# A fused attention and expert kernel: first loads issued by three engines, zero matmuls at the start, the first two tiles closed earlier, and GpSimd's sums in pieces

## The chip, the cores and the metric

The kernel runs on one core of a Trainium2 chip. The metric is the device time of one execution in microseconds. Engines are named as the profile names them: PE is TensorE (with PEld for its weight loads), DVE is VectorE, ACT is ScalarE, POOL is GpSimd and SP is SyncE.

## What is computed

A sliding-window attention is followed by a layer of eight experts, of which each token goes to one. All is in float32.

```python
# q, k, v: (8, 8, 576, 64); window 64
scores = matmul(q, k.T) / sqrt(64);  mask = (rel >= 0) & (rel < 64)
attn = softmax(where(mask, scores, -1e9));  x = (attn @ v) as 4608 tokens x 512
logits = x @ w_gate;  expert = argmax(logits);  gate = softmax(logits)[expert]
for e in range(8):                       # w1: (8, 512, 1024), w2: (8, 1024, 512)
    y[tokens of e] = relu(x[tokens of e] @ w1[e]) @ w2[e]
out = gate * y
```

## The kernel before

**Attention.** The batch is cut into four groups of two sequences (bg = 0 to 3), each group into four units (one pair of heads), each unit into three rounds. That gives N = 48 rounds, and `step(s)` is a software pipeline over them: it scores round s + 1, weighs v for round s - 1, turns (transposes) the q and k of round s + 3, and does whatever stands in `todo` for s. The last 64 positions of each sequence, the "rests", are loaded for a whole group at once and are used by each unit's third round.

```python
def step(s):
    if 0 <= s + 1 < N:
        prs[s + 1] = softened(*masked(s + 1, scored(s + 1)))   # PE, DVE (L585), ACT (L595)
    if 0 <= s - 1 < N:
        px = weighted(s - 1, pTs.pop(s - 1))                   # PE (L618)
    ripe = 0 <= s - 3 < N and logit(s - 3)                     # PE (L655)
    if 0 <= s < N:
        pTs[s] = flipped(prs.pop(s))                           # PE (L603), DVE and ACT (L605)
    if 0 <= s - 1 < N:
        divided(s - 1, px)                                     # DVE (L628 to L632)
    ...                                                        # at each unit's first step: loads for u+2 and u+3
    if s + 3 < N:
        turned(s + 3)                                          # PE (L539, L531), ACT (L544, L534)
    if 0 <= s - 2 < N:
        x_turned(s - 2)                                        # PE (L643), ACT (L646)
    for op in todo.pop(s, ()):
        op()
    ...
load_qk(0); (wg and zrow); load_rests(0); load_v(0); load_qk(1); load_v(1); load_qk(2)   # all on SyncE
for s in range(-3, N):
    step(s)
```

`load_v` also has GpSimd copy each v to a second alignment (L511 to L517).

**Routing.** When a group's logits are known, `choose(bg)` (DVE) finds each token's expert and its rank among that expert's tokens; `place` (DVE, L746) makes a one-hot operand of the rank; `weigh` multiplies x by the gate; `store` writes x to DRAM. A tile is 256 tokens of one expert, in two halves of 128. The table that says which token stands in which slot is a series of small matmuls of those operands. Tiles 0 and 1 belong to expert 0 and are closed before the last group: the count of expert 0 is raised to 512 after the third group. Their table is made in step 45, and the tokens are fetched with an indirect DMA:

```python
def first_tiles():                       # todo of step N - 3
    V.scalar_tensor_tensor(out=key[:], ...)                    # L859
    V.tensor_tensor(out=hi_e[:], ..., op=ALU.is_equal)         # L862
    for j in range(NJE):                                       # 27 x 2 matmuls, L869
        for i in range(2):
            nc.tensor.matmul(slots, lhsT=lo[:, i, j], rhs=hi_e[:, j], ...)
    V.tensor_scalar(out=perm_e[:], in0=slots, ...)             # L872
    gather_first(perm_e[:, 0:C])                               # GpSimd: fill with zeros, indirect DMA
```

**Experts.** A tile goes through `turn` (transpose x), `sums_x`, `hidden` (x @ w1, relu) and `output` (@ w2). Both products are done with seven half-size products in place of eight, which needs sums of the quarters of x (DVE, L311), of w1 and w2 (GpSimd, L139) and of the hidden layer (DVE, L139):

```python
def left_sums(eng, s, a11, a12, a21, a22):
    for n, (a, b, op) in enumerate((
        (a21, a22, ALU.add), (s[:, 0], a11, ALU.subtract), (a11, a21, ALU.subtract),
        (a12, s[:, 1], ALU.subtract))):
        yield partial(eng.tensor_tensor, out=s[:, n], in0=a, in1=b, op=op)   # L139
def sums_w1(e): form(left_sums(G, s1s[e % NW], *w1q(e)))
def sums_w2(e): form(right_sums(G, s2s[e % NW], *w2q(e)))
```

After the loop of steps, tile 0's products are interleaved with the last group's routing and with the table of all further tiles (`slot_table`, matmuls L807). Then tile 1 follows, and a loop over the experts.

Of the kernel before, what the change touches and what calls it, by code (L numbers as in the profile page):

```python
# [4 lines left out]

# [31 lines left out]
def kernel(  # L37
# [44 lines left out]

    ident = consts.tile([P, P], F32, name="ident")
    make_identity(nc, ident[:])
    GE = 32
# [54 lines left out]

    def w1q(e):
        w = w1s[e % NW]
        return [w[:, a * HG : (a + 1) * HG, f * HD : (f + 1) * HD] for f in range(2) for a in range(2)]
# [5 lines left out]
    def sums_w1(e):  # L149
        form(left_sums(G, s1s[e % NW], *w1q(e)))  # L150

    def sums_w2(e):
        form(right_sums(G, s2s[e % NW], *w2q(e)))
# [59 lines left out]
    hi_e = rt.tile([P, NJE, NE * C], BF16, name="hi_e")  # L213
# [23 lines left out]
    ST = 3  # L237
# [39 lines left out]
    def gather_first(tokens):  # L277

        for c in range(C):
            G.memset(xg[c], 0.0)  # L280

            G.indirect_dma_start(
                out=xg[c], out_offset=None, in_=x_dram[0 : NT - BG * S, :],
                in_offset=bass.IndirectOffsetOnAxis(ap=tokens[:, c : c + 1], axis=0),
                bounds_check=NT - BG * S - 1, oob_is_err=False,
            )
# [12 lines left out]
    def turn():  # L299

        for c in range(C):
            for g in range(NG):
                nc.tensor.transpose(out=tps[c][:, g, :], in_=xg[c][:, g * P : (g + 1) * P], identity=ident[:])  # L303
            nc.scalar.copy(out=xq[:, :, c], in_=tps[c].rearrange("p (a g) s -> p a g s", a=2))
        yield

    def sums_x():

        b12, b22, b21 = tps[1][:, 0:HG], tps[1][:, HG:], tps[0][:, HG:]
        for n, (a, b) in enumerate(((b12, xq[:, 0, 0]), (b22, xs[:, 0]), (b22, xq[:, 0, 1]), (xs[:, 1], b21))):  # L310
            V.tensor_tensor(out=xs[:, n], in0=a, in1=b, op=ALU.subtract)  # L311
# [128 lines left out]
    with tc.manual_schedule(), ExitStack() as held, ExitStack() as brief:  # L440
# [6 lines left out]


        NM = 2 + ST
        mask = consts.tile([P, NM, P], BF16, name="mask")  # L450
        nc.gpsimd.memset(mask[:], 0.0)
        for h in range(2):
            for m0, m1, first in ((0, 1, False), (1, 2, h == 0), (2, NM, False)):
                rows = slice(h * D, (h + 1) * D)
                sel = partial(
                    nc.gpsimd.affine_select, out=mask[rows, m0:m1, :], in_=mask[rows, m0:m1, :], fill=MASKED,
                )
                if first:
                    sel(pattern=[[0, m1 - m0], [-1, P]], compare_op=ALU.is_ge, base=0, channel_multiplier=1)
                else:  # L460
                    sel(pattern=[[0, m1 - m0], [1, P]], compare_op=ALU.is_gt, base=0, channel_multiplier=-1)
                    sel(pattern=[[0, m1 - m0], [-1, P]], compare_op=ALU.is_ge, base=WINDOW, channel_multiplier=1)
# [18 lines left out]
        def load_qk(u):  # L481
            bg, g = units[u]
            qks[u] = [qk_m(((u % 3 + 2) % 3 * 2 + n) * 1024, BG, NV, 2, D) for n in range(2)]
            for i in range(BG):
                for t, src in zip(qks[u], (q, k)):
                    for h in range(2):
                        nc.sync.dma_start(
                            out=t[:, i, :, h, :],
                            in_=src[bg * BG + i, 2 * g + h, 0:SM, :].rearrange("(p j) d -> p j d", j=NV),
                        )  # L490

        def load_rests(bg):

            at = 6144 + bg % 2 * 2048
            vr = qk_m(at + 1024, BG, H, D)
            rests[bg] = [qk_m(at, H, D), qk_m(at + 512, H, D), vr]
            for t, src in zip(rests[bg], (q, k)):
                for i in range(BG):
                    nc.sync.dma_start(
                        out=t[i * D : (i + 1) * D], in_=src[bg * BG + i, :, SM:S, :].rearrange("h p d -> p h d")  # L500
                    )
            for i in range(BG):
                nc.sync.dma_start(out=vr[D:P, i], in_=v[bg * BG + i, :, SM:S, :].rearrange("h p d -> p h d"))
# [173 lines left out]
        def choose(bg):  # L677
# [50 lines left out]
            if bg == last - 1:  # L728

                V.tensor_scalar_max(count[:, 0:1], count[:, 0:1], float(NE * TB))  # L730
# [48 lines left out]
        def slot_table(hi):  # L779
# [29 lines left out]
            for j in range(NJE):  # L809
                fill(j)  # L810
            for n in range(NST):
                for m in range(ST):
                    place(NJE + n * ST + m)
                yield
# [18 lines left out]
        def after(s, routing, bg):  # L833
# [14 lines left out]
            for n in (0, 0, 1, 2, 2):  # L848
                do(n, part)
            for m in range(NTB):  # L850
                do(3 + m // 3, partial(place, bg * NTB + m))
                do((2, 2, 3, 3, 4, 4, 4, 5, 5)[m], partial(weigh, bg, m, nc.scalar if m in (2, 6) else G))
                if m % ST == ST - 1:
                    do(3 + m // ST, partial(store, bg, m // ST, G))
            do(6, first_tiles)

        def first_tiles():

            V.scalar_tensor_tensor(  # L859
                out=key[:], in0=rkhi[:, 0:NJE], scalar=1.0, in1=oh_all[:, 0, 0:NJE], op0=ALU.add, op1=ALU.mult  # L860
            )
            V.tensor_tensor(  # L862
                out=hi_e[:], in0=_inner(key[:], NE * C), in1=_ins(hi_id[:, C + 1 : C + 1 + NE * C], 1, NJE),
                op=ALU.is_equal,
            )
            slots = banks[next(tr_ring)](0, NE * C)
            for j in range(NJE):
                for i in range(2):
                    nc.tensor.matmul(  # L869
                        slots, lhsT=lo[:, i, j], rhs=hi_e[:, j], start=(i + j == 0), stop=(i + j == NJE)  # L870
                    )
            V.tensor_scalar(out=perm_e[:], in0=slots, scalar1=-1.0, scalar2=float(NT), op0=ALU.mult, op1=ALU.add)  # L872
            gather_first(perm_e[:, 0:C])

        N = NU * NST
        load_qk(0)
        nc.sync.dma_start(out=wg[:, :, 0:E], in_=moe_w_gate.rearrange("(g p) e -> p g e", p=P))
        nc.sync.dma_start(out=x_dram[NT : NT + 1, :], in_=zrow[:])
        load_rests(0)
        load_v(0)  # L880
        load_qk(1)
        load_v(1)
        load_qk(2)

        for g in range(NG):
            step = NST * (g // 2) + g % 2 + 1
# [3 lines left out]
        for n, op in enumerate(left_sums(G, s1s[0], *w1q(0))):  # L890
# [5 lines left out]
        def step(s):  # L896
            if 0 <= s + 1 < N:
# [8 lines left out]
            if s >= 0 and s % NST == 0:  # L906
# [5 lines left out]
                if u + 3 < NU:  # L912
                    load_qk(u + 3)
# [15 lines left out]
        for n, s in enumerate((N - 6, N - 3)):  # L929
            fs = slice(n * HF, (n + 1) * HF)  # L930
            todo.setdefault(s, []).append(partial(nc.sync.dma_start, out=w2s[0][:, fs], in_=w2v[0][:, fs]))
        for s in range(-3, N):
            step(s)
        assert not todo
        sums_w2(0)
# [4 lines left out]
        tile0 = chain(hidden(0), turn(), output(0))  # L940
        px = weighted(N - 1, pTs.pop(N - 1))
        form_all(turn())
# [3 lines left out]
        sums_x()  # L946
        gather_first(perm_e[:, C : 2 * C])
        by_tok = [by_tokens(last, c) for c in range(NST)]
        next(by_tok[0])
        next(tile0)  # L950
        logit(N - 2)
        x_turned(N - 1)
        next(by_tok[0], None)
# [23 lines left out]
        next(tile0)  # L977
        next(routing, None)
        weigh_some(2)
# [4 lines left out]
        for _ in range(8):  # L984
            next(tile0)
            next(table, None)
        assert next(tile0, None) is None
# [82 lines left out]
```

## Time and profile before

| | before |
|---|---|
| median of 3 runs | 763.73 us (763.55 to 766.46) |
| span of the profiled execution | 763.5 us |
| busy PE, PEld, DVE, ACT, POOL | 722.8, 651.8, 397.0, 268.3, 357.0 us |
| first matmul starts | 4.63 us |
| turn of tile 0 starts | 216.48 us |
| wait of TensorE ahead of L869 | 2.70 us |
| a GpSimd sum of w1 or w2 (128 x 1024) | 2.35 us |

The page of the profile gives each engine's busy time, then the span in 40 slices (19 us each) with the busy share in tenths. A timeline line has the start in us, the duration in us, the engine, the line of the kernel, the operation, output <- inputs, shape and count; a bracket at its end is the idle time of the engine ahead of it and what ended it. A line of waits has the engine and what it was to do, what it waited for, the sum in us, how often, and the longest.

### The profile page before, as it was taken

Reading aid. Unit: us, or ns where it says so; the run is one execution under the profiler, and the core shown is the slowest. Engines: PE = TensorE matmul, PEld = TensorE weight load, DVE = VectorE, ACT = ScalarE, POOL = GpSimd, SP = SyncE. Lnnn points to the kernel's source line nnn. Section 1 sums busy time; section 2 is a strip of 40 time slices with the busy share of each in tenths; the row PEclk is TensorE's granted clock in tenths of the full one; section 3 lists DMA queues with packets and bytes.
Section 4 is the critical chain, followed back from the end, with each engine's and each line's share of the span. In section 5 each row is a group of like instructions: output and inputs, shape, how many; then the busy total and the mean of one; then the engine's idle time right before and its main releaser. Section 6 shows DMA issues by size and latency. Waiting matters only on the chain. (4 is left out here: it accounts for less than half of the span.)

```text
span 763.5 us, 18251 instructions
## 1 busy us (share of the span) xinstructions
PE 722.8 (95%) x7018; PEld 651.8 (85%) x7018; DVE 397.0 (52%) x1355; ACT 268.3 (35%) x676; POOL 357.0 (47%) x366
## 2 busy tenths in 40 slices
PE   5999999998899989999999999999999999999995
PEld 3878888887688978988999899899998899988994
DVE  2666998988748554434533452352434452424432
ACT  4778888897634201211220121111220121202220
POOL 5214668485770544546531553663256465262111
PEclk9999999999899999999999999999999999999998
DMA  7998889794513711702501170441161171101101
GB/s 161 210 201 183 190 183 257 175 236 128 181 56 125 276 57 32 264 29 93 203 32 54 48 257 30 141 164 56 44 247 53 35 258 56 41 25 42 43 28 55
DMA packets 137616, 94.48 MB, mean 124 GB/s; under 512 B 117072, under 2 KB 117072, under 8 KB 137490
## 3 DMA queue, kind: packets, MB, share of 16 engines
q1 hardware_dynamic: 127858, 62.16, 29.6%
q0 software_dynamic: 9056, 28.58, 11.3%
q10 hardware_dynamic: 576, 2.10, 0.9%
q8 instruction: 74, 1.21, 0.6%
q14 instruction: 52, 0.43, 0.2%
HBM read 73.94 MB, written 20.45 MB: 124 GB/s over the span
## 5 line engine op out<-in xcount | busy, mean ns | idle before, releaser
L322 PE MATMUL bank<-qk_m,s 128*128 128x128 f32 x1216 | 145.6, 275 | 0.0
L322 PEld LDWEIGHTS bank<-qk_m,s 128*128 128x128 f32 x1216 | 140.5, 192 | 0.1
L322 PE MATMUL bank<-qk_m,w 128*128 128x128 f32 x912 | 112.5, 276 | 10.7 <-DVE v_m L358 7.1
L272 POOL DMA_INDIRECT qk_m<-x_dram,at_g x42 | 44.6, 1061 | 166.3 <-PE bank L303 159.0
L322 PEld LDWEIGHTS bank<-qk_m,w 128*128 128x128 f32 x912 | 106.8, 192 | 15.9 <-issue 15.7
L595 ACT ACTIVATE pr<-pr,mx 128x128 f32<-128x128 f32 x288 | 89.7, 391 | 34.2 <-DVE mx L585 31.8
L358 DVE TENSOR_TENSOR v_m<-bank,v_m 128x256 f32<-128x256 f32 x101 | 40.9, 422 | 110.3 <-PE bank L362 54.8
L585 DVE CUSTOM_DVE_ANT_0 pr<-bank,mask 128x128 f32<-128x128 f32 x288 | 64.4, 286 | 28.2 <-PE bank L572 25.8
L292 POOL DMA_INDIRECT out_dram<-v_m,at_s x42 | 42.4, 1009 | 60.7 <-DVE v_m L358 49.0
L329 ACT COPY qk_m<-bank 128x512 f32<-128x512 f32 x19 | 11.2, 587 | 164.2 <-PE bank L322 135.0
L139 POOL TENSOR_TENSOR s<-w 128x1024 f32<-128x1024 f32 x22 | 52.3, 2377 | 17.6 <-DMA qk_m<-x_dram,at_g 17.6
L362 PE MATMUL bank<-qkT_m,v_m 128*128 128x256 f32 x240 | 54.0, 380 | 1.7 <-DVE v_m L139 1.7
L362 PEld LDWEIGHTS bank<-qkT_m,v_m 128*128 128x128 f32 x240 | 45.4, 190 | 8.6 <-DVE v_m L139 2.5
L513 POOL COPY v_m<-v_m 64x520 f32<-64x520 f32 x32 | 19.8, 618 | 69.3 <-DMA v_m<-in_v_dram 55.1
L362 PE MATMUL bank<-qk_m 128*128 128x256 f32 x224 | 52.1, 380 | 0.0
L618 PEld LDWEIGHTS bank<-v_m,pT 128*64 128x64 f32 x1152 | 41.2, 140 | 11.7 <-DVE xs L632 5.5
L618 PE MATMUL bank<-v_m,pT 128*64 128x65 f32 x1152 | 48.0, 231 | 2.7 <-DVE xs L632 2.7
L362 PE MATMUL bank<-s,v_m 128*128 128x256 f32 x216 | 48.1, 379 | 0.0
L362 PEld LDWEIGHTS bank<-qk_m 128*128 128x128 f32 x224 | 41.5, 190 | 5.5 <-ACT v_m L374 0.4
L362 PEld LDWEIGHTS bank<-s,v_m 128*128 128x128 f32 x216 | 41.0, 190 | 5.6
L572 PE MATMUL bank<-qkT_m 64*64 64x128 f32 x1152 | 45.4, 289 | 0.1
L539 PE MATMUL bank<-ident,qk_m 128*128 128x128 f32 x256 | 35.9, 283 | 8.5 <-DMA qk_m<-in_q_dram 6.3
(167 smaller groups left out, 1223.8 us busy)
## 6 DMA issues: line engine op xcount, KB each, us to landing
w<-in_moe_w_dram SPq DMA_DIRECT2D x11, 2048.0 KB, 9.4
qk_m<-in_q_dram SPq DMA_DIRECT2D x72, 128.0 KB, 3.4
qk_m<-in_k_dram SPq DMA_DIRECT2D x72, 128.0 KB, 3.4
v_m<-in_v_dram SPq DMA_DIRECT2D x64, 128.0 KB, 3.8
qk_m<-in_moe_w_dram SPq DMA_DIRECT2D x3, 2048.0 KB, 15.3
x_dram<-xs POOLq DMA_DIRECT2D x6, 512.0 KB, 4.7
x_dram<-xs POOLq DMA_DIRECT2D x3, 768.0 KB, 5.0
w<-in_moe_w_dram ACTq DMA_DIRECT2D x4, 512.0 KB, 4.4
```

What stands on the lines that cost most here:

```text
L139: op()
L272: G.indirect_dma_start(out=xg[c], out_offset=None, in_=x_dram[:, :], in_offset=bass.IndirectOffsetOnAxis(ap=at_g[:, c : c + 1], axis=0),)
L292: put = G.indirect_dma_start(out=out[:, :], out_offset=bass.IndirectOffsetOnAxis(ap=at_s[:, c : c + 1], axis=0), in_=ys[c], in_offset=None ...
L322: nc.tensor.matmul(acc[:, f, :], lhsT=a[:, g, f * P : (f + 1) * P], rhs=b[:, g, :], start=(first and f == 0 and g == 0), stop=(g == HG - 1 ...
L358: plus = lambda out, a, b: V.tensor_tensor(out=out, in0=a, in1=b, op=ALU.add)
L362: nc.tensor.matmul(acc, lhsT=a[:, f, :], rhs=b[:, f, :], start=(start and f == 0), stop=(stop and f == HF - 1), skip_group_check=True,)
L513: nc.gpsimd.tensor_copy(out=vb[0:D, i].rearrange("p j h d -> p (j h d)"), in_=va[D:P, i].rearrange("p j h d -> p (j h d)"),)
L539: nc.tensor.transpose(out=tr.rearrange("d a b -> d (a b)").rearrange("d (p j) -> d j p", j=NV)[:, j, :], in_=t[:, c, j].rearrange("p h d - ...
L572: nc.tensor.matmul(out_, lhsT=qT[rows, t, a * WINDOW : (a + 1) * WINDOW], rhs=rhs, start=True, stop=True, skip_group_check=True,)
L585: V.tensor_tensor_reduce(out=prs[h][:, m, :], in0=scs[h][:, m, :], in1=mask[:, m0 + m, :], scale=-scale, scalar=-2 * MASKED, op0=ALU.add, ...
L595: nc.scalar.activation(out=y, in_=y, func=AF.Exp, scale=-1.0, bias=mx[:, h, m : m + 1])
L618: nc.tensor.matmul(px[a * D : (a + 1) * D, h, m, :], lhsT=pTs[h][:, m, a * D : (a + 1) * D], rhs=vt[:, h, :], start=True, stop=True, skip_ ...
```

## The change

It has four parts. The first loads are spread over SyncE, ScalarE and GpSimd, and the first rounds are ordered so that round 0 is scored as soon as its first tiles are turned; the masks are made earlier, and nine matmuls of zeros keep TensorE occupied while the first loads are under way. Tile 0 is closed after two groups and tile 1 after three, each with a table of its own, so that tile 0's tokens are fetched and turned while attention still runs. GpSimd's sums of weights are cut into four pieces each, so that they hold up other engines for less at a time. The routing of the third group is spread over more steps, and the filling of the later tiles' table is moved. Cut to its core:

```diff
+    warm = consts.tile([P, 4 * P], BF16, name="warm")
+    nc.vector.memset(warm[:], 0.0)
+    (the masks are made here, ahead of the other constants)
+    def pieces(engine):
+        def tensor_tensor(op, **aps):
+            n = aps["out"].shape[-1] // 4
+            for i in range(4):
+                engine.tensor_tensor(op=op, **{name: ap[:, :, i * n : (i + 1) * n] for name, ap in aps.items()})
-        form(left_sums(G, s1s[e % NW], *w1q(e)))
+        form(left_sums(pieces(G), s1s[e % NW], *w1q(e)))
-        form(right_sums(G, s2s[e % NW], *w2q(e)))
+        form(right_sums(pieces(G), s2s[e % NW], *w2q(e)))
-            if bg == last - 1:
-                V.tensor_scalar_max(count[:, 0:1], count[:, 0:1], float(NE * TB))
+            if last - NE <= bg < last:
+                V.tensor_scalar_max(count[:, 0:1], count[:, 0:1], float((bg - last + NE + 1) * TB))
     (slot_table)
-            for j in range(NJE):
-                fill(j)
             for n in range(NST):
                 for m in range(ST):
                     place(NJE + n * ST + m)
+                if n == 1:
+                    for j in range(NJE):
+                        fill(j)
                 yield
     (the routing of the third group)
-            for n in (0, 0, 1, 2, 2):
+            for n in (0, 1, 1, 2, 3):
                 do(n, part)
             for m in range(NTB):
-                do(3 + m // 3, partial(place, bg * NTB + m))
-                do((2, 2, 3, 3, 4, 4, 4, 5, 5)[m], partial(weigh, bg, m, nc.scalar if m in (2, 6) else G))
+                do((4, 4, 5, 5, 6, 6, 7, 7, 7)[m], partial(place, bg * NTB + m))
+                do((2, 3, 3, 4, 4, 5, 5, 6, 6)[m], partial(weigh, bg, m, G))
                 if m % ST == ST - 1:
-                    do(3 + m // ST, partial(store, bg, m // ST, G))
-            do(6, first_tiles)
+                    do(4 + m // ST, partial(store, bg, m // ST, nc.sync))
-        def first_tiles():
+        def first_tile(n):                 # nj = 18 groups of 128 tokens for tile 0, 27 for tile 1
+            (key and hi_e for nj groups); yield
+            (nj * 2 matmuls); (perm_e); gather_first(to, nj * P); yield
-        load_qk(0)
-        (wg, zrow)
-        load_rests(0)
-        load_v(0)
-        load_qk(1)
+        load_qk(0, nc.sync, nc.sync)
+        load_rests(0, 0, 2, nc.scalar, nc.sync)     # heads 0 and 1: q, k by ScalarE, v by SyncE
+        load_v(0)
+        load_qk(1, nc.sync, nc.sync)
+        load_rests(0, 2, H, G)                      # the other heads by GpSimd
+        (wg, zrow)
         load_v(1)
-        load_qk(2)
+        load_qk(2, nc.sync, nc.sync)
-            step = NST * (g // 2) + g % 2 + 1        # the four loads of the first w1, by ScalarE
+            step = NST * (1 + g // 2) + g % 2 + 1
-        for n, s in enumerate((N - 6, N - 3)):       # the two halves of the first w2
+        for n, s in enumerate((N - 7, N - 4)):
-        for s in range(-3, N):
+        tile0 = chain(hidden(0), turn(), output(0))
+        first = first_tile(0)
+        todo.setdefault(N - 10, []).append(partial(next, first))
+        todo.setdefault(N - 9, []).append(partial(next, first))
+        free = [banks[i](0, NG, P) for i in (0, 1)]
+        todo.setdefault(N - 2, []).extend((lambda: form_all(turn(free)), partial(sums_x, free)))
+        todo.setdefault(N - 1, []).extend((partial(next, tile0), partial(sums_w2, 0)))
+        for _ in range(9):
+            nc.tensor.matmul(banks[7](0, 4 * P), lhsT=warm[:, 0:P], rhs=warm[:], start=True, stop=True)
+        turned(0)
+        first = masked(0, scored(0))
+        turned(1)
+        prs[0] = softened(*first)
+        for s in range(N):
             step(s)                                  # step 0 also does turned(2)
-        sums_w2(0)
     (after the loop)
-        form_all(turn())
-        sums_x()
-        gather_first(perm_e[:, C : 2 * C])
+        second = first_tile(1)
+        next(second)                                 # key and hi_e of tile 1
+        next(tile0)
         ...
+        next(second)                                 # its matmuls and its gather
```

After this, a few of tile 0's products and one weighing of the last group stand a place later or earlier than before.

## The prediction

> **What bounds the kernel now.** I read the summary first, then the busy time by stretch, then TensorE's own waits, and only then the timeline of the places that these named.
>
> ```profile
> PE 722.8 (95%) x7018; PEld 651.8 (85%) x7018; DVE 397.0 (52%) x1355; ACT 268.3 (35%) x676; POOL 357.0 (47%) x366
> PE   5999999998899989999999999999999999999995
> DMA  7998889794513711702501170441161171101101
> ```
>
> TensorE is busy 95% of the span, so the prize is at most its idle time, 763.5 - 722.8 = 40.7 us, plus what it spends on slow matmuls. The slices say where: the first one is half empty, the next nine are nearly full while the DMA engines are too, and the last is half empty because of the final scatter, which this change leaves alone.
>
> ```profile
> 5.00:10.00 5.00, 4.08 (x20) 2.63 (x22) 0.00 (x0) 1.82 (x4) 2.58 (x7) 1.00 0.74 158
> 10.00:15.00 5.00, 3.73 (x51) 2.54 (x51) 1.35 (x12) 2.64 (x8) 0.29 (x1) 1.00 1.00 201
> 15.00:20.00 5.00, 3.04 (x30) 2.29 (x30) 1.82 (x13) 3.04 (x9) 2.83 (x6) 1.00 1.05 204
> 160.00:200.00 40.00, 37.18 (x665) 30.72 (x659) 36.12 (x192) 33.08 (x98) 28.14 (x32) 1.00 0.64 188
> 200.00:240.00 40.00, 35.78 (x397) 31.54 (x395) 25.12 (x98) 19.04 (x45) 20.46 (x17) 0.91 0.36 124
> ```
>
> The columns are PE, PEld, DVE, ACT and POOL, granted clock, DMA share and GB/s. TensorE's idle time is 5.6 us in the first 10 us, 3.2 in the next 10, 2.8 in 160 to 200 and 4.2 in 200 to 240. From 400 us to 720 us each 40 us hold only 0.7 to 1.1 us of it: the experts' loop has little left to win. In 160 to 200 VectorE is busy 36.1 of 40 us, nearly as much as TensorE.
>
> ```profile
> PE bank L539 <- DMA qk_m<-in_q_dram: 6.3, 3, 4.6
> PE bank L869 <- DVE hi_e L862: 2.7, 1, 2.7
> PE bank L643 <- DVE pT L605: 2.0, 2, 1.4
> PE bank L362 <- DVE v_m L139: 1.7, 2, 0.9
> PE bank L807 <- DVE qk_m L311: 1.3, 1, 1.3
> ```
>
> These are the waits of TensorE that the change can touch: the first loads, the table of the first tiles (L869), VectorE falling behind at the end of attention (L643), and two later ones. The fourth is one collision:
>
> ```profile
> 263.71 2.35 POOL L139 TENSOR_TENSOR s<-s,w 128x1024 f32<-128x1024 f32 x1
> 263.89 2.71 DVE L139 TENSOR_TENSOR v_m<-qk_m 128x512 f32<-128x512 f32 x1 [0.75 <-ACT qk_m L350]
> 292.58 0.69 DVE L139 TENSOR_TENSOR v_m<-qk_m 128x512 f32<-128x512 f32 x1 [0.70 <-ACT qk_m L350]
> ```
>
> The same VectorE sum takes 0.69 us alone and 2.71 while GpSimd has a sum of 2.35 under way. The last view is the matmuls' speed:
>
> ```profile
> 9.83 1.56 PE L572 MATMUL bank<-qkT_m 64*64 64x128 f32 x24
> 24.57 0.89 PE L572 MATMUL bank<-qkT_m 64*64 64x128 f32 x24
> 206.19 1.56 PE L572 MATMUL bank<-qkT_m 64*64 64x128 f32 x24
> ```
>
> Twenty-four score products take 1.56 us at the start, 0.89 once TensorE has been kept busy, and 1.56 again at 206.19, after the idle 2.7 us. So a wait is paid twice.
>
> **What the Trainium skill says.** "TensorE: Matmul & The Clock Gate", Part 1, has the array at half rate until about 3.4 us of sustained work, and at half rate again after an idle window of that length. The trace agrees in size (1.56 against 0.89) and shows both directions; here 2.70 us of idle time were enough. "SBUF — State Buffer", Who interferes with whom, says that a VectorE instruction with two SBUF inputs and a GpSimd instruction that reads SBUF exclude one another for a whole instruction. The collision above agrees: 2.71 is close to a GpSimd sum's 2.35 plus part of the own 0.69. "Trainium Kernel Development and Optimization", Key Constraints, says that the queues of SyncE, ScalarE and GpSimd feed the same 16 DMA engines, and that issuing from several saves only issue time. The trace has SyncE issuing without a pause to about 80 us, at some 0.65 us for a 128 KB load, with the DMA share at 1.00 to 1.05 between 10 and 20 us. That caps the start's gain.
>
> **The start.** Removed from SyncE ahead of the first tiles: four loads of the rests of q and k (now in ScalarE's and GpSimd's queues) and the two small ones (wg and the zero row, 0.55 and 0.36 us, now later). The loads of v and of unit 1 begin after 8 + 2 + 4 issues: 0.8 + 8 x 0.67 + 2 x 0.65 + 2.3 = about 9.8 us, against 13.80 before. In the trace the first q of unit 1 is turned at 17.96, 4.2 us after its issue, and its k ends at 19.10. So 4.0 us is the gain if landing still takes as long. It will not quite: up to 19 us some 2.9 MB land at about 200 GB/s, and GpSimd's share of the rests (0.6 MB, 3 us of the DMA engines) now competes. What helps is that the first 10 us, with 40 and 74% DMA share, fill better. I choose 3.5 us. The masks (4.3 us of GpSimd's time) come before the other constants and end near 6.3 us; the first score product can be masked near 8.5 us instead of 11.57. Nine zero matmuls (128 x 512; that page gives 426.7 ns for one of 512 columns at the half rate, so 3.8 us together, an estimate) run between 1.2 and 5 us, where TensorE waits anyway. They may make TensorE warm, which saves up to 1.6 us in the step at 19.66 to 23.60 (3.94 us against 2.33 for the same three groups later); but until about 57 us SyncE's stream of loads paces the kernel (unit 4 is waited for at 54.9 and 56.3), so most of this would be handed to a DMA wait. The first w1's loads, moved three steps later, relieve the stream early and load it later. **Start: 3.5 us.**
>
> **The end of attention.** Step s is a round of the attention loop, 48 in all, about 4.1 us each. Before, the table of both tiles is built in step 45: 2.70 us idle, 54 small matmuls (1.58 us, 29 ns each), and then cold matmuls; from 206.19 to 211.13 four groups take 4.94 us that take 2.67 warm, 2.3 us lost. In the last two steps, without new tiles to turn, TensorE idles 0.62 and 0.88 us. After, tile 0's table (36 matmuls, 1.05 us) stands in step 39, its key made a step earlier, so it waits for little. Tile 1's 54 matmuls come after the loop: moved, not removed. The turn of tile 0 (8 transposes, 1.04 us) and its first product (16 matmuls, 1.95 us) move into steps 46 and 47, where the idle 1.5 us was. If all went: 2.70 + 2.3 + 1.5 - 1.05 = 5.4 us. But VectorE is why TensorE waited. From step 39 it has about 25 us of attention, 4.3 of routing, 18 placings that take 0.3 us alone and 0.7 beside GpSimd's weighing (together 8 to 9), and now tile 0's sums of x (4 x 0.41): about 40 us, where the stretch lasted some 43.5. Placings are spread over four steps instead of three, which helps. I take 4.7 us of the 5.4. **End of attention: 4.7 us.**
>
> **Tile 0 and the slot table.** Filling the table for the first three groups moves behind two rounds of placing, so the 1.29 us before L807, while VectorE makes the table's operand, goes: **1.3 us.**
>
> **Sums in pieces.** A sum of 2.35 us becomes four of 0.59 plus a gap of 0.1 (the trace has 0.09 between two sums): about 0.7 each, 2.8 in place of 2.4 a sum, 3 us more of GpSimd per expert, out of an expert's 53 us in which it is half idle. A VectorE sum then waits for at most one piece, 1.3 us and not 2.7, so the second and third sums of 264 to 272 are ready before TensorE asks: **1.7 us.** The single collisions later (3.27 us at 321, 374, 453) are off TensorE's path already and give nothing.
>
> Both closings of a tile leave the number of tiles alone: expert 0 has 421 tokens in the first two groups and 538 in three, counted from the inputs, so neither 256 nor 512 pads anything, and its six half tiles stay six.
>
> Sum: 3.5 + 4.7 + 1.3 + 1.7 = 11.2 us. 763.7 - 11.2 = 752.5; I put 752 us, since a warm start may keep a part of its 1.6.
>
> **Rivals.** First, the start is bound by the DMA engines, not by issue: then three queues share the same 200 GB/s, the first k of unit 1 lands near 17 us, and 1.5 to 2 us are gained; 754. For it speak the share of 1.0; against it the 40% in the first 5 us. GpSimd's own loads stand behind its copies of v, which wait for landings, so they may also come so late that the rest of unit 1 (turned near 23 us) is waited for. Second, VectorE becomes the bound from step 39 to the end, and the end gives 3 us or less; 755. Its 36.1 of 40 us speak for it. Third, GpSimd becomes the bound: its sums of w2 (now 11 us) stand before tile 1's gather. I have the gather landing about 3 us before tile 1 is turned; if w2's second half lands late, TensorE waits 2 to 5 us there, and goes cold. Fourth, the good side: warm from the first product and no DMA wait gives 5 to 6 us at the start; 748 or 749.
>
> **Range and chances.** The start may be 2 to 6, the end 2.5 to 5.5, the two others together 1.5 to 3.5. These are partly independent: 747 to 757 should hold it 8 times in 10. The 2% line is 748.5, which needs nearly every part at its best. Slower by 2% would need a new wait of 25 us, of which I see no sign.
>
> **What would show each step.** Right: unit 1's first k turned near 15.5 us; score products of 0.89 us from the second group at the latest; no wait before the tables' matmuls (L869 before) and none of 1.56 us near 200; tile 0 turned inside the loop, about 8 us or more before 216.48; VectorE's sums of tile 1 at no more than about 1.4 us each; the end of the loop's first expert 11 us earlier and the later experts as long as before. Wrong: waits for q or k between 20 and 57 us that sum to over 2 us, VectorE waits of over 3 us between steps 39 and 47, a wait before tile 1's turn, or experts that each take longer because GpSimd's pieces delay its scatters and gathers.

## The result and the profile after: 6.7% slower

The changed kernel takes 816.05 us (813.73 to 818.56), the kernel before 764.35 beside it: a ratio of 1.067, 95% interval 1.063 to 1.071. The prediction was 752.0.

The page of the changed kernel, with the lines that answer to the first ones shown of before, and the two groups of sums:

```profile
PE 741.2 (91%) x7063; PEld 662.3 (81%) x7063; DVE 450.8 (55%) x1360; ACT 266.4 (33%) x674; POOL 386.2 (47%) x560
PE   7979999998799998699699979979996997999996
DMA  8998788774225416116110521521160160101101
L159 DVE TENSOR_TENSOR v_m<-qk_m,v_m 128x512 f32<-128x512 f32 x19 | 80.5, 4237 | 0.0
L166 POOL TENSOR_TENSOR s<-w 128x256 f32<-128x256 f32 x96 | 67.1, 732 | 18.7 <-DMA qk_m<-x_dram,at_g 18.6
```

The first slice of TensorE is fuller (7 for 5; the zero matmuls, 4.02 us, count in it), but from the 17th slice on there are six new dips (6, 6, 7, 7, 6, 7). VectorE is busy 54 us longer with five instructions more, and one group holds nearly all of it: 19 sums of 128x512 take 4237 ns on average, where before the same 19 took 1500. TensorE's own waits in the changed kernel (line of the matmul, what it waited for; us in total, times, longest):

```profile
PE bank L389 <- DVE v_m L385: 34.9, 6, 5.8
PE bank L349 <- DVE v_m L385: 10.2, 13, 1.3
PE bank L551 <- DMA qk_m<-in_k_dram: 5.8, 4, 2.7
PE bank L655 <- DVE pT L617: 2.6, 2, 2.3
```

The waits for the first tiles' table and for the slot table are gone, as planned. In their place stand six waits of 5.8 us in the second layer of the experts. The timeline of one of them:

```profile
327.53 11.84 DVE L159 TENSOR_TENSOR v_m<-qk_m,v_m 128x512 f32<-128x512 f32 x1
327.86 2.79 POOL L166 TENSOR_TENSOR s<-w 128x256 f32<-128x256 f32 x4
330.59 2.76 POOL L166 TENSOR_TENSOR s<-s,w 128x256 f32<-128x256 f32 x4
333.32 2.76 POOL L166 TENSOR_TENSOR s<-w 128x256 f32<-128x256 f32 x4
336.05 2.76 POOL L166 TENSOR_TENSOR s<-w,s 128x256 f32<-128x256 f32 x4
341.20 3.64 PE L389 MATMUL bank<-w,v_m 128*128 128x256 f32 x8 [5.81 <-DVE v_m L385]
```

VectorE's sum begins 0.3 us ahead of GpSimd's sixteen pieces and ends 0.6 us after the last of them. TensorE waits 5.81 us and then runs cold (at a granted clock of 0.50), 3.64 us for eight matmuls that take 1.89 warm: 7.6 us, six times, 45 us.

To say where time went, I cut a run at four marks of its trace: the scores of round 39, the first put of tile 0 (a put is an indirect DMA into the output), the last put of tile 1, the first put of the last tile.

| | before | changed |
|---|---|---|
| scores of round 2 / 10 | 19.7 / 51.7 | 15.7 / 48.3 |
| scores of round 12 / 39 | 61.2 / 168.0 | 63.2 / 170.2 |
| A: round 39 to tile 0's put | 85.9 | 88.9 |
| B: to tile 1's last put | 26.5 | 24.3 |
| C: to the last tile's put | 475.7 | 525.5 |
| last product to the end | 9.3 | 7.9 |

The loop (C) costs 49.8 us. A gain of 3.4 us at the start is gone by round 12, and the end of attention (A) costs 3.0 us where 6.0 had been promised.

### The profile page after: what moved, and what is told of

It is laid out like the page before. It is cut to its first block, busy times and chain, and to the rows that moved or that the text cites. A ratio compares the mean times of both kernels' runs of the same rounds, so it can differ in the third digit from the quotient of the medians.

```text
span 814.9 us, 18562 instructions
## 1 busy us (share of the span) xinstructions
PE 741.2 (91%) x7063; PEld 662.3 (81%) x7063; DVE 450.8 (55%) x1360; ACT 266.4 (33%) x674; POOL 386.2 (47%) x560
## 5 line engine op out<-in xcount | busy, mean ns | idle before, releaser
L159 DVE TENSOR_TENSOR v_m<-qk_m,v_m 128x512 f32<-128x512 f32 x19 | 80.5, 4237 | 0.0
L166 POOL TENSOR_TENSOR s<-w 128x256 f32<-128x256 f32 x96 | 67.1, 732 | 18.7 <-DMA qk_m<-x_dram,at_g 18.6
L359 DVE TENSOR_TENSOR qk_m<-bank,qk_m 128x512 f32<-128x512 f32 x19 | 13.1, 692 | 59.8 <-PE bank L349 55.1
```

The costliest lines, as they stand in the source:

```text
L166: engine.tensor_tensor(op=op, **{name: ap[:, :, i * n : (i + 1) * n] for name, ap in aps.items()})
```

## Experiments on the sums in pieces

**The change with whole sums** (`no_pieces`), and **the kernel before with pieces** (`pieces_alone`).

```diff
 # no_pieces; pieces_alone has the removed lines in the kernel before
-            for i in range(4):
-                engine.tensor_tensor(op=op, **{... quarter i ...})
+            engine.tensor_tensor(op=op, **aps)
```

> The changed kernel with GpSimd's sums whole again, all else kept. Theory (pieces let a stream of GpSimd hold the shared way to SBUF without a gap, and starve one VectorE sum for 11.8 us in six experts): the six sums fall from 11.85 to about 3.3 us, TensorE's 34.9 us of waits ahead of the products of w2 go, and with the slow matmuls behind them some 48 us: 767 us. Rival (GpSimd simply has too much to do, or the earlier closing of tiles disturbs the loop): 800 us or more remain.

> The kernel before with nothing but the sums in pieces. Theory: the whole loss of the experts' loop is here, about 764 + 48 - 2 = 810 us, with six VectorE sums of about 11.8 us and the collision at tile 1 solved (about 1.2 us each in place of 2.7). Rival (pieces only hurt together with the other parts): within 5 us of 764.

Measured: 767.11 us (ratio 1.0055, 1.0034 to 1.0076) and 802.45 (1.0521, 1.0481 to 1.0561). Without pieces C is 475.3 us and the six sums take 3.26 to 3.28; with pieces alone five sums take 11.82 to 11.84 (the sixth, at 525 us, is done before GpSimd's stream begins) and C is 515.1. So the pieces are the large loss, by themselves; and the rest of the change without them gains nothing.

**Why.** A whole first sum is followed by a second that reads what the first wrote, and the trace of before has 0.08 us between them (321.85 + 2.38 to 324.31), where VectorE got in:

```profile
321.53 3.26 DVE L139 TENSOR_TENSOR v_m<-qk_m,v_m 128x512 f32<-128x512 f32 x1
321.85 2.38 POOL L139 TENSOR_TENSOR s<-w 128x1024 f32<-128x1024 f32 x1
324.31 2.70 POOL L139 TENSOR_TENSOR s<-s,w 128x1024 f32<-128x1024 f32 x1
```

In pieces, none needs what the one just ahead wrote (the second sum's pieces need the one four back, the fourth's the one eight back), and the stream has no gap. Three kernels test that. In `pieces_by_column` the pieces are the same, but the four sums of one quarter come in turn, so of each four pieces the second needs what the one just ahead wrote. In `fourth_sum_later` VectorE's sum arrives in the stream's middle and not ahead of it. In `whole_1324` nothing is cut: the kernel before has its four whole sums in another order, which moves the gap from behind the first to behind the third.

```diff
 # pieces_by_column (n is a quarter of the columns; the sums of w2 likewise)
-        form(left_sums(pieces(G), s1s[e % NW], *w1q(e)))
+        for i in range(4):
+            cut = slice(i * n, (i + 1) * n)
+            form(left_sums(G, s1s[e % NW][:, :, :, cut], *(a[:, :, cut] for a in w1q(e))))
 # fourth_sum_later
-        form(left_sums(V, hs, a11, a12, a21, a22))
+        *three, fourth = left_sums(V, hs, a11, a12, a21, a22)
+        form(three)                              # fourth() stands behind sums_x()
 # whole_1324, in the kernel before
-        form(left_sums(G, s1s[e % NW], *w1q(e)))
+        ops = list(left_sums(G, s1s[e % NW], *w1q(e)))
+        form(ops[n] for n in (0, 2, 1, 3))
```

> The changed kernel with as many pieces of the same size, but in another order: all four sums of the first quarter of the columns, then of the second, and so on, so that the second sum of a quarter reads what the instruction just ahead of it wrote. If VectorE's interrupted sum gets on at the first gap in GpSimd's stream, and a sum that needs the one just ahead makes such a gap, the six sums take about 1.4 us and the kernel 765 us. Rival (small pieces starve VectorE by their number or size): still about 11.8 us, 815 us.

> The changed kernel, pieces kept, with VectorE's fourth sum of the hidden layer moved behind the four sums of x, so that it begins some 1.5 us after GpSimd's stream has begun and not 0.3 us ahead of it. If only an instruction that is interrupted while under way is starved, and one that arrives later takes its turn after one piece (as at tile 1, 0.8 to 1.2 us), it takes at most 1.4 us and the kernel 766 us. Rival (any VectorE sum of two SBUF inputs waits until a gapless stream ends): it takes about 10 us and the kernel stays above 800 us.

> The kernel before with GpSimd's four whole sums of w1 in the order first, third, second, fourth: the same instructions and sizes, but each of the first three now needs nothing that the one just ahead of it wrote, so the gap that stood after the first stands after the third. Gap theory: VectorE's sum that meets them in the experts' loop lasts until the third of GpSimd's sums ends, 7.5 to 8.5 us in place of 3.27, TensorE waits some 2 to 3 us for it in each of six experts, and the time is 776 to 782 us. Rival (only pieces starve it, because they are small or many): 3.3 us each and 764 us.

Measured: 763.48 us (1.0000, 0.9985 to 1.0015), 810.98 (1.0627, 1.0600 to 1.0654) and 779.48 (1.0196, 1.0134 to 1.0259); C is 471.2, 518.9 and 492.0. The timeline of `pieces_by_column`:

```profile
325.10 1.65 DVE L159 TENSOR_TENSOR v_m<-qk_m,v_m 128x512 f32<-128x512 f32 x1
325.44 0.75 POOL L159 TENSOR_TENSOR s<-w 128x256 f32<-128x256 f32 x1
326.27 1.07 POOL L159 TENSOR_TENSOR s<-s,w 128x256 f32<-128x256 f32 x1
```

The sum gets in at the gap of 0.08 us behind the first piece and takes 1.65 us. In `fourth_sum_later` and in `whole_1324` the same sum:

```profile
322.34 10.37 DVE L409 TENSOR_TENSOR v_m<-qk_m,v_m 128x512 f32<-128x512 f32 x1
```

```profile
320.92 7.87 DVE L139 TENSOR_TENSOR v_m<-qk_m,v_m 128x512 f32<-128x512 f32 x1
321.26 4.67 POOL L139 TENSOR_TENSOR s<-w 128x1024 f32<-128x1024 f32 x2
325.87 2.36 POOL L139 TENSOR_TENSOR s<-s,w 128x1024 f32<-128x1024 f32 x1
```

In the last one VectorE stands for three whole sums, to the first gap (325.87 + 2.36 = 328.23, then 0.56 us of its own). So, in the loop, it is the missing gap and neither the size nor the number of the pieces. The idea behind `fourth_sum_later`, that only an instruction caught under way is shut out, fell: one that arrives later waits just as well to the end of the stream.

**What is not explained.** At tile 1 the same pieces let VectorE in after each (the changed kernel again):

```profile
269.16 0.80 DVE L159 TENSOR_TENSOR v_m<-qk_m 128x512 f32<-128x512 f32 x1 [0.75 <-ACT qk_m L377]
272.15 1.21 DVE L159 TENSOR_TENSOR v_m<-qk_m,v_m 128x512 f32<-128x512 f32 x1
268.68 4.13 POOL L166 TENSOR_TENSOR s<-s,w 128x256 f32<-128x256 f32 x4
```

Whole sums do the same at tile 1 of the kernel before: GpSimd's third ends at 268.81 with no gap to the fourth, and VectorE's sum that met it still ends at 269.36. In the loop the stream follows directly on the issue of two gathers; here it does not. `sums_before_gather` moves the sums ahead of the gathers. `sums_behind` leaves the order and lets the stream begin only when VectorE's fourth sum is done.

```diff
 # sums_before_gather, in body()
         form_all(turn())
+        for n in ahead:                          # the next expert
+            sums_w1(n)
         gather(perm_i[:, after])
 # sums_behind
+                G.tensor_copy(out=seen[:], in_=hs[:, 3, 0, 0:1])
                 sums_w1(e + 1)
```

> The change, with GpSimd's sums in pieces for the next expert put ahead of the two gathers of the tile in place of behind them. The stream then follows on a scatter issued long before, and VectorE's four sums meet it in its middle. If a gather issued directly ahead is what shuts VectorE out, its sums get in after each piece as at tile 1, 0.8 to 1.3 us each, and the time is 766 to 775 us. Rival (the pieces shut VectorE out in the loop in any case): one of its sums lasts until the stream ends, 6 to 11 us in six experts, and the time is 800 us or more.

> The change, with one copy of one column (128x1) on GpSimd ahead of its sums, which reads VectorE's fourth sum of the second layer, so that the stream of pieces begins only when that sum is done. Theory (the meetings are the whole loss): all six sums take 0.70 us, TensorE's 5.8 us waits go, and the time is 762 to 767 us, that of the change with whole sums (767) or up to 4 us less. Rival (the stream of pieces costs TensorE elsewhere as well): over 770 us.

Measured: 769.96 us (1.0058, 1.0034 to 1.0082) and 771.74 (1.0096, 1.0072 to 1.0119). With the sums ahead of the gathers, and so behind the puts, VectorE gets in after each piece in four experts (sums of up to 1.22 us), but in two it is shut out to the stream's end, and C is 483.4:

```profile
371.90 1.08 DVE L159 TENSOR_TENSOR v_m<-qk_m 128x512 f32<-128x512 f32 x1 [0.70 <-ACT qk_m L377]
503.15 5.91 DVE L159 TENSOR_TENSOR v_m<-qk_m 128x512 f32<-128x512 f32 x1 [0.70 <-ACT qk_m L377]
```

In three of the four open experts GpSimd had waited 0.57 to 0.86 us between the put and its sums; in the fourth, and in the two that shut VectorE out, the sums followed the put at once. So an indirect DMA directly ahead of the stream matters, and it is not all: what decides whether a stream without gaps opens at a piece's end stays open. `sums_behind` missed its time but settles the account: all its sums take 0.69 us and C is 475.8, that of whole sums, so the meetings were the whole loss in the loop. Its 771.74 us are not the loop's: most of the excess is in B, 32.1 us in place of 24.3: at tile 1 GpSimd now waits 4.83 us for VectorE, and the put behind its sums comes later. My expectation had left tile 1 out.

## Experiments on the start

**The start alone** (`start_alone`), and with w1's loads later (`start_late_w1`).

```diff
-            step = NST * (1 + g // 2) + g % 2 + 1          # w1's loads
+            step = NST * (5 + g // 2) + g % 2 + 1
-            todo.setdefault(3 * NST + n, []).append(op)     # GpSimd's sums of it
+            todo.setdefault(9 * NST + n, []).append(op)
```

> The kernel before with the start alone: zeros on TensorE, the masks first, the loads of the first unit from three engines, w1 three steps later; GpSimd's sums whole and the end of attention as before. Theory A (bandwidth): the start gains 3.5 to 4 us at the second step of scores, and gives back 1 to 4 us of it at the fourth unit, because w1's loads now fall beside that unit's q and k while the DMA engines are at 0.96 to 1.0 of their time; the last weighted group comes 0 to 3 us sooner than in the kernel before, and the time is 761 to 764 us. Rival B (the start is worth its whole size): the last weighted group comes 3.5 us sooner, the time is 760.0 us. A wait on in_k_dram or in_q_dram beyond 50 us speaks for A, none for B.

> The same start, with the four loads of w1 a further twelve steps later (near 80 to 95 us) and GpSimd's four sums of it eighteen steps later. Theory A (w1's 2 MB compete with the fourth unit's q and k): no wait on q or k beyond 30 us, the whole start gain of 3.5 to 4 us is there at step 11 and at the last weighted group, and the time is 759.5 to 761 us, 1 to 3 us under the start alone. Rival B (the later waits are not from w1): the wait of 1 to 3 us at 50 to 60 us stays, and the time is that of the start alone within 1 us.

Measured: 765.20 us (1.0015, 1.0002 to 1.0027) and 766.63 (1.0031, 1.0019 to 1.0043). Round 10 is scored 3.7 and 4.2 us sooner than before. At round 12 the nine profiled kernels with the start as changed lie from 3.3 us sooner to 5.3 later than before. Up to there they differ only in whether the first w1's sums are whole or in pieces, and both kinds spread: TensorE has single waits of 0.7 to 3.4 us there on the q and k of unit 4, or none. With w1's loads later it is 5.5 us sooner, without such a wait (the two other kernels with later loads: 5.3 and 6.2), and most of it lasts to round 32 (135.0 for 140.0). So w1's transfers most likely competed there; GpSimd's sums of w1 moved with them, and the two were not separated. But the gain is lost at rounds 33 to 35, 15.4 us for 8.2: the sums moved along, and met VectorE's routing of the second group, and TensorE waits 4.3 us for VectorE once. `start_columns` has w1's loads at rounds 9 to 13, its sums from 14 on, and the pieces by column.

> The start of the change with w1's loads at steps 9, 10, 12 and 13 (44 to 62 us, behind the fourth unit's loads) and the sums of it at steps 14 to 17, and the pieces by column; the end of attention as before. If the start's gain is only lost where transfers or GpSimd's sums then collide, no wait on q or k beyond 30 us exceeds 1.3 us, step 39 stands 3.5 to 5 us sooner than in the kernel before, and the time is 757 to 760 us. Rival: the gain is lost again at another place before step 39, 761 to 764 us.

767.92 us (1.0057, 1.0036 to 1.0079): again 5.3 us sooner at round 12, and 6 us lost at rounds 21 to 24. The same happens in `all_mended`, a version told of below, whose start is the same. Its timeline:

```profile
91.73 2.28 DVE L750 TENSOR_TENSOR r_rank<-r_rank,oh_all 128x72 f32<-128x72 f32 x1
94.05 0.29 DVE L753 TENSOR_REDUCE r_pos<-r_rank 128x9 int32<-128x72 f32 x1
94.37 1.89 DVE L755 TENSOR_SCALAR r_half<-r_pos 128x9 int32<-128x9 int32 x1
96.29 2.26 DVE L756 CAST rkhi<-r_half 128x9 f32<-128x9 int32 x1
98.59 0.17 DVE L757 TENSOR_SCALAR r_half<-r_pos 128x9 int32<-128x9 int32 x1
```

While GpSimd's three whole sums run (91.56 to 98.53), a VectorE operation on nine columns takes 1.89 us; after them one of the same size takes 0.17. "SBUF — State Buffer", Who interferes with whom, names the kinds: sums of two SBUF operands, and copies, casts and tensor_scalar in their fast modes, but not a reduction. The trace agrees: the reduction at 94.05 takes its 0.29 us.

## Experiments on the end of attention

**The closings alone** (`end_alone`); then with VectorE's routing in its old steps and GpSimd's weighings moved behind it (`end_mended`).

```diff
 # end_mended against end_alone
-            for n in (0, 1, 1, 2, 3):                       # choosing
+            for n in (0, 0, 1, 2, 2):
-                do((4, 4, 5, 5, 6, 6, 7, 7, 7)[m], partial(place, ...))
-                do((2, 3, 3, 4, 4, 5, 5, 6, 6)[m], partial(weigh, bg, m, G))
+                do(3 + m // 3, partial(place, ...))
+                do(5 + m // 3, partial(weigh, bg, m, nc.scalar if m in (2, 6) else G))
                 ...                                         # stores on SyncE, and sums_w2(0) after the last step
```

> The kernel before with the two closings, their routing and the later fill of the slot table alone; start and GpSimd's sums as before. Theory A: the closings move VectorE's choosing and placing beside nine weighings of GpSimd in a row, and cost 3 to 4 us between step 39 and the first product of tile 1 (84.8 us in place of 81.6), so the time is 766 to 768 us. Rival B (the prediction): the closings save 4.7 us plus 1.3 us at the slot table, 758 us. Rival C: the loss at the end is only there when the start also shifts the phases; then 764 us.

> The two closings, with VectorE's choosing and placing in the steps that they had before (0, 0, 1, 2, 2 and 3 to 5), GpSimd's weighings moved behind them (steps 5 to 7, two on ScalarE as before), and the sums of w2 after the last step as before; start and sums as before, sums whole. Theory A (the loss at the end is VectorE slowed by GpSimd): choosing's operations take 0.17 to 0.3 us again in place of 0.5 to 0.8, no placing takes over 1 us, the 9 us of losses there go, the wait for the table of tile 0 (2.7 us) is gone, and the first product of tile 1 starts 79 to 81.5 us after the scores of step 39 in place of 86.9; the time is 760 to 764 us. Rival (the closings lose for another reason, such as the table's matmuls or the gather): 84 us or more there, 767 us or more.

Measured: 772.72 us (1.0096, 1.0070 to 1.0121) and 766.57 (1.0035, 1.0021 to 1.0049); A is 91.1 and 87.1, against 85.9. Four us of either time are of another kind: from TensorE's last product to the end they take 13.3 us, before takes 9.3, because GpSimd's last long DRAIN (an instruction near the end of its queue) takes 10.0 us and not 3.4. That is so in each kernel with 100 transfers issued by GpSimd; with 106 or 112 it takes 3.4 or 4.6. Why stays open. The timeline of `end_alone` shows the rest:

```profile
185.87 13.89 POOL L757 TENSOR_SCALAR xs<-xs,gate 128x512 f32<-128x512 f32 x9
188.31 0.73 DVE L726 TENSOR_TENSOR r_rank<-r_inc,count 128x72 f32<-128x72 f32 x1
208.13 2.34 POOL L139 TENSOR_TENSOR qkT_m<-qk_m 128x1024 f32<-128x1024 f32 x1
208.14 2.38 DVE L746 TENSOR_SCALAR lo<-lane,low,tok_b 128x128 bf16<-128x128 bf16 x1
```

GpSimd weighs nine times in a row, just when VectorE chooses: operations of 0.2 us take 0.5 to 0.8. The placings, moved later, meet the sums of w2, and four of them take 2.2 to 2.4 us in place of 0.3. In `end_mended` no placing takes over 0.31 us any more, but the choosing is still slow (r_rank 0.59 to 0.80), and TensorE waits 6.1 us for VectorE once: I had moved the weighings to later steps, but GpSimd runs ahead of the steps and began them at 183.54 all the same.

The kernel before has a brake there. Its third weighing is ScalarE's, and the store of it stands in GpSimd's queue, so GpSimd waits 8 us while VectorE chooses. `before_unpaced` takes the brake from the kernel before; `end_paced` gives it back to the closings, with every step as before.

```diff
 # before_unpaced
-                do((2, 2, 3, 3, 4, 4, 4, 5, 5)[m], partial(weigh, bg, m, nc.scalar if m in (2, 6) else G))
+                do((2, 2, 3, 3, 4, 4, 4, 5, 5)[m], partial(weigh, bg, m, G))
-                    do(3 + m // ST, partial(store, bg, m // ST, G))
+                    do(3 + m // ST, partial(store, bg, m // ST, nc.sync))
 # end_paced against end_mended
-                do(5 + m // 3, partial(weigh, bg, m, nc.scalar if m in (2, 6) else G))
+                do((2, 2, 3, 3, 4, 4, 4, 5, 5)[m], partial(weigh, bg, m, nc.scalar if m in (2, 6) else G))
-                    do(5 + m // ST, partial(store, bg, m // ST, nc.sync))
+                    do(3 + m // ST, partial(store, bg, m // ST, G))
```

> The kernel before with all nine weighings of the last but one group on GpSimd and their stores on SyncE, as in the change; nothing else changed. In the kernel before, the third weighing is ScalarE's and GpSimd's queue holds its store behind it, so GpSimd stands still for 8 us while VectorE chooses. Theory A (GpSimd's row slows VectorE's choosing): the choosing operations from r_inc to low take 0.5 to 0.8 us each in place of 0.17 to 0.3, and the last weighted group stands 2 to 5 us later counted from step 39; the time is 766 to 770 us. Rival (the closings themselves are the loss): 763.5 to 765 us, with the operations slowed or not.

> The two closings alone, with choosing, placing, weighings and stores exactly in the steps and on the engines of the kernel before, and the sums of w2 after the loop. Theory A: choosing runs at 0.17 to 0.3 us an operation, the wait of 2.7 us for the table is gone, the first product of tile 1 starts 77 to 80 us after the scores of step 39 (81.6 in the kernel before), and the time is 759.5 to 762.5 us. Rival (closings lose by themselves): 83 us or more there, 766 us or more.

Measured: 767.74 us (1.0049, 1.0033 to 1.0066) and 760.10 (0.9947, 0.9929 to 0.9965). The first looks like the theory and is not: A is 83.6, less than before, TensorE's last product comes 1.5 us sooner than before, and the whole excess is the long DRAIN. A row of weighings alone slows only some of the choosing there (four operations of 0.55 to 0.64). `end_paced` is what the closings can give: A is 82.3, 3.6 us less than before, and the time 3.6 us less. (A is read from one execution each; over the seven kernels that end attention as the kernel before does it lies between 84.5 and 85.9.) Its row of weighings is broken:

```profile
185.52 3.12 POOL L757 TENSOR_SCALAR xs<-xs,gate 128x512 f32<-128x512 f32 x2
194.84 0.86 POOL L766 DMA_DIRECT2D x_dram<-xs  x1 [6.20 <-ACT pr L595]
```

Two operations of choosing meet the first two weighings (0.73 and 0.61 us); those from 187.90 on take 0.17 to 0.29. `end_paced` and `end_mended` differ in the steps of the weighings and in the stores alone, so that is worth 4.8 us of A; the other edits from `end_alone` to `end_mended` (choosing and placing in the old steps, w2's sums after the loop, two weighings on ScalarE) are worth 4.0. Why the same row does harm behind the closings' gathers and little in the kernel before isn't settled; it resembles the sums that follow on a gather.

## Versions

`by_column_alone` is the kernel before with the pieces by column; `all_mended` joins `end_mended`, the start of `start_columns` and the columns; `start_end_paced` joins the change's start with `end_paced`; `all_paced` adds the columns to that.

> The kernel before with GpSimd's sums of w1 and w2 in the loop cut into the same quarters, but all four sums of one quarter in turn, so that every second piece needs what the one just ahead of it wrote; start and end of attention as before. Theory A (gaps): VectorE's sum takes 1.65 us in place of 3.27 in each of six experts, none of it starves, and the pieces are worth what the prediction gave them and somewhat more, since the whole sums also held VectorE at tile 1: 760.5 to 762.5 us. Rival (the 3.27 us are off TensorE's path): 763.5 to 764.5 us.

> All three together: the start with w1's loads later, the pieces by column, and the closings with VectorE's routing kept clear of GpSimd. If the parts add up: 754 to 758 us, under both kernels. If the closings bring nothing even so: 757 to 761 us, that of the start with the columns.

> The change's start and closings with that pacing, GpSimd's sums whole. If the start's 3 to 4 us and the closings' 2 to 4 us add up: 757 to 760 us. If the start's gain is lost again somewhere before step 39: 760 to 763 us.

> The same with the pieces by column. The pieces by column alone brought nothing to the kernel before (ratio 1.0016) and took 3.6 us off the change: so 754 to 760 us, within 1 us of the same with whole sums if they are off TensorE's path, 2 to 4 us less if not.

| | us | ratio, 95% interval |
|---|---|---|
| by_column_alone | 765.46 | 1.0016, 1.0004 to 1.0029 |
| all_mended | 764.73 | 1.0013, 1.0000 to 1.0026 |
| start_end_paced | 760.17 | 0.9945, 0.9927 to 0.9964 |
| all_paced | 762.25 | 0.9975, 0.9957 to 0.9993 |
| end_paced (above) | 760.10 | 0.9947, 0.9929 to 0.9965 |

The best are the paced closings, with or without the start: 0.5% under the kernel before. The columns bring the kernel before nothing. C is 2.9 us shorter, but only because its first mark, tile 1's last put, comes 3.2 us later: from the first of the six sums to the last sum of the kernel it takes 425.0 us, before 423.5. So VectorE's sums of 3.27 us were off TensorE's path, as the prediction had it. The put is late because GpSimd's stream lasts 13.2 us (260.93 to 274.13) and the next gather and put stand behind it in its queue. In the change the columns took 3.6 us off the whole sums (763.48 for 767.11), and in the profiles A is 3.4 us shorter (85.7 for 89.1), where the placings meet the sums of w2. The start brings nothing in the median either; in the profile of `start_end_paced` round 39 stands at 170.1.

## Why the prediction was wrong, step by step

- **Sums in pieces: the step that failed.** It said that a VectorE sum "then waits for at most one piece, 1.3 us". At tile 1 that held (0.80 to 1.21 us; B is 2.2 us less, 1.7 predicted). In the loop, behind the gathers, the sum waited for all sixteen pieces, 11.84 us, and TensorE lost some 7.6 us six times; C is 49.8 us longer. It also said that the single collisions there "are off TensorE's path already and give nothing". That was right for 3.27 us (cut to 1.65 they leave the loop as long) and wrong as a reason to pass over them, since I kept them at their old length. The list of what would make the prediction wrong named the pieces, but for GpSimd's scatters and gathers.
- **Slower by over 2%** was set aside, since it "would need a new wait of 25 us, of which I see no sign". The sign was in the view: the collision of 3.27 us is about 0.69 and one whole sum of 2.35, and a gap of 0.08 us behind that sum is all that ended it.
- **Start, 3.5 us: right as far as it was worked out.** Unit 1's first k is turned at 15.19 (15.5 predicted), the zero matmuls took 4.02 us (3.8 estimated), the scores up to round 10 take 0.89 us, but for 1.41 in round 1, and round 10 is scored 3.4 us sooner. But "three steps later, relieve the stream early and load it later" had no number, and there the gain goes. The sign that I named, over 2 us of waits for q or k between 20 and 57 us, came: 2.22, 1.25 and 2.67 us. The first leaves the scores at 0.89 us, the last makes them cold again (1.56). The rival of transfers as the bound was right in kind, later than it said.
- **End of attention, 4.7 us, and slot table, 1.3 us: the waits went, the time did not.** No wait stands ahead of either table, and tile 0 is turned inside the loop, though at 215.20 and not 8 us before 216.48. The second rival, VectorE as the bound, came true, beyond the 3 us that it gave: A is 3.0 us more. I had counted placings at "0.7 beside GpSimd's weighing" but left the choosing at its undisturbed 4.3 us, while its operations took 0.5 to 0.8 us in place of 0.2, and did not see that placings moved later meet w2's sums: in the changed kernel one takes 2.69 us and eight 0.7 to 0.9, and with whole sums four take 2.2 to 2.4. With the old pacing the closings and the later fill of the slot table give 3.6 of the 6.0 us.
- **The experts' tiles** are as many as before (42 puts in both), as the prediction had it.

## What to carry to other kernels

Before work on GpSimd is cut or moved, list which VectorE operations it will now meet, and treat a GpSimd stream that stands directly behind an indirect DMA as one block up to its next dependency on the instruction just ahead: more pieces need not give VectorE more turns. A queue that waits for another engine can be a useful brake: behind the closings' gathers, 6 us in which GpSimd stood still kept it off VectorE's serial work (in the kernel before, A lost nothing when its 8 us were taken away), and steps in the program don't pace an engine that can run ahead. Where many transfers follow each other, a gain at the start counts only once the next load that is waited for comes sooner too.

## What the runs showed of the hardware that I had not expected

- GpSimd's sixteen gapless pieces shut a VectorE sum of two SBUF operands out for 11.84 us. "SBUF — State Buffer", Who interferes with whom, has the second engine blocked for a whole instruction of the first; here it was sixteen, and a gap of about 0.08 us ended it in `pieces_by_column`. At tile 1, with no gather just ahead, the same stream opened after each piece.
- VectorE operations that read one operand from PSUM were not slowed beside the pieces: 0.41 to 0.42 us for 128x256 at tile 1 as elsewhere.
- GpSimd's last long DRAIN takes 3.4, 4.6 or 10.0 us by the program: `end_mended` was done with its products 1.5 us sooner than before and ended 2.5 us later.
